# A linear attention and tanh-shrink MLP kernel: copies of v moved, epsilon ahead of den, transposes one step later, and the last output tile over two queues

## The chip, the cores and the metric

A run uses one core of one Trainium2 chip. The metric is the device time of one execution in microseconds. A profiled execution gives a span that is some 1.8 us shorter than the time of the same execution (294.0 and 295.8 for the kernel before). VectorE is called DVE in the profile, TensorE PE, ScalarE ACT and GpSimd POOL.

## The reference, cut to what matters

```python
q, k, v: (8, 8, 576, 64) f32      # batch, heads, sequence, head width
q_p, k_p = phi(q), phi(k)         # phi(x) = where(x > 0, x, exp(x) - 1) + 1
kv  = einsum('bhsd,bhse->bhde', k_p, v);  z = sum(k_p, axis=2)
num = einsum('bhsd,bhde->bhse', q_p, kv)
den = einsum('bhsd,bhd->bhs', q_p, z)[..., None] + 1e-06
x   = (num / den)                 # to (4608, 512): batch and sequence by heads and width
h   = x @ w_in                    # (4608, 512) @ (512, 2048)
out = (h - tanh(h)) @ w_out       # (4608, 2048) @ (2048, 512)
```

## The kernel before: the parts that matter

The 4608 rows are done in nine stages of 512 (c = 0 to 8). A stage is L1 (x @ w_in, 16 steps of four matmuls, then tanh on ScalarE and the subtraction on VectorE into `gT`) and L2 (`gT` @ w_out, 16 steps of four matmuls). The attention of the batches to come is hung into these steps: `s1[n]` after step n of L1, `s2[n]` after step n of L2. TensorE, VectorE, ScalarE and GpSimd are each given their own instructions in this program order. In the first stage L2 goes by quarters of w_out: steps 0 to 3 read the first quarter for the four output tiles, steps 4 to 7 the second, and so on.

```python
def a_kv(b, banks):                     # k'v and z by 192 columns: v and a block of ones
    ...                                 # 36 matmuls of 64x192, v_b holds v and the ones
def a_kv_cols(b, banks):                # by 136 columns: 128 of v, 8 of ones, from the copy vp
    ...                                 # 36 matmuls of 64x136
def a_vp(b, i):                         # the copy of v that a_kv_cols reads
    nc.vector.tensor_copy(vp[:, i, :, 0:128].rearrange(...), v_b[b % 2][:, 0:2, i])

# all loads are issued by GpSimd, in this order
load_q(0); load_k(0); load_v(0); [load_wi(g) for g in range(4)]
load_k(1); load_wo(0); load_q(1); ...; load_wo(1); load_v(1); load_wo(2)

# first stage (c == 0)
s2[1]: a_qphi(1, 1), load_q(2), load_wo(3), load_k(2), load_v(2)
s2[3]: a_qT_pe(1, 0)                    # transposes of q of batch 1, first half (nine on TensorE)
s2[4]: a_qT_pe(1, 1)                    # second half
s2[5]: b0_scale_rest, prepare;  s2[6]: a_kv(1);  s2[8]: a_den(1) ...
s2[15]: a_kphi(2, 0)
# second stage (c == 1)
s1[1]: a_kphi(2, 1);  s1[6]: a_kv(2);  s1[9]: a_den(2)
# each stage from c == 1 to 5: at s2[8] the copies of the batch after next, then num
s2[8]: a_qphi(n2, 1), a_qT_dma(n2), a_vp(n2, 0), a_vp(n2, 1)
s2[9..13] (c == 1: 11..15): a_num(n1, p)     # eviction by VectorE, two PSUM banks in turn
```

Of the kernel before, what the change touches and what calls it, by code (L numbers as in the profile page):

```python
# [18 lines left out]
def kernel(  # L19
# [9 lines left out]
    nc = tc.nc  # L29
    B, H, S, D = q.shape  # L30
    N = B * S
    DM = H * D
    DF = moe_w_in.shape[1]
    NP = H // 2
    NF = DF // 128
    NC = N // 512
    J = S // 64
# [105 lines left out]
    def a_kphi(b, i):  # L143
        phi(b, k_t, kp_t, "kp", i)

    def a_qphi(b, i):
        phi(b, q_t, qp_t, "qp", i)
# [4 lines left out]
    def a_qT_dma(b):  # L152
        new_qT(b)
        nc.sync.dma_start_transpose(
            out=qT_t[b].rearrange("p i j g t -> p (i j) (g t)"),
            in_=qp_t[b].rearrange("p i j h d -> p (i j h d)"))

    def a_qT_pe(b, i, banks, on=None):
        if i == 0:
            new_qT(b)  # L160
        for n in range(2):
            j0, j1 = ((0, 5), (5, 9))[n]
            ps = banks().bitcast(BF16).rearrange("p (j t) -> p j t", t=128)
            for j in range(j0, j1):
                nc.tensor.transpose(ps[:, j - j0, :], qp_t[b][:, i, j].rearrange("p h d -> p (h d)"), ident)  # L165
            src = ps[:, 0:j1 - j0, :]
            dst = qT_t[b][:, i, j0:j1].rearrange("p j g t -> p j (g t)")
            if (on or "AV")[n] == "A":
                nc.scalar.copy(dst, src)
            else:  # L170
                nc.vector.tensor_copy(dst, src)
# [14 lines left out]
        for hg in range(2):  # L186
            nc.vector.tensor_mul(kz_t[b][:, hg], ps[hg][:, :, 0:160], mask[:, hg])

    def a_vp(b, i):
        nc.vector.tensor_copy(vp[:, i, :, 0:128].rearrange("p j (h d) -> p h j d", h=2), v_b[b % 2][:, 0:2, i])  # L190

    def a_kv_cols(b, banks):
        kp = kp_t[b]
        kz_t[b] = kz_c[b % 2]
        ps = [banks()[:, 0:272].rearrange("p (i e) -> p i e", i=2) for hg in range(2)]
        for i in range(2):
            for j in range(J):
                for hg in range(2):
                    r = slice(64 * hg, 64 * hg + 64)
                    nc.tensor.matmul(ps[hg][:, i, :], kp[r, i, j].rearrange("p h d -> p (h d)"),  # L200
                                     vp[r, i, j, :], start=(j == 0), stop=(j == J - 1))
        for hg in range(2):
            nc.vector.tensor_mul(kz_t[b][:, hg, :, 0:136], ps[hg], mask[:, hg, :, 0:136])
# [61 lines left out]
            xT[:, :, 512:576].rearrange("p a (t c) -> p a t c", t=4),  # L265
            ps[:, 0:NP, :].rearrange("p a (t c) -> p a t c", t=4), rdb_t[0])

    def a_den(b, banks):

        kz, qT = kz_t[b], qT_t[b]  # L270
        ps = banks()[:, 0:J * 16]
        for n, p in enumerate((0, 2, 1, 3)):
            for t in range(4):
                nc.tensor.matmul(ps[32 * t:32 * t + 32], kz[:, p // 2, p % 2, 128:160],  # L274
                                 qT[:, p % 2, :, p // 2, 16 * t:16 * t + 16],
                                 start=(n == 0), stop=(n == NP - 1 and b > 0))
        for t in range(4) if b == 0 else ():
            nc.tensor.matmul(ps[32 * t:32 * t + 32], eps[:, 0:32], one[:, 0:J * 16], start=False, stop=True)
        if b > 0:
            den = rpool.tile([128, J * 16], F32, name="den")  # L280
            nc.vector.tensor_scalar(den, ps, 1e-6, None, ALU.add)
        else:
            den = ps
        rden = rpool.tile([128, J * 16], F32, name="rden")
        nc.vector.reciprocal(rden, den)  # L285
        rden_t[b] = rden
# [97 lines left out]
    def evac(c, i, o, f0=0, f1=None):  # L384
        f1 = DM if f1 is None else f1
        osb = opool.tile([128, DM], F32, name="osb")
        nc.scalar.copy(osb[:, f0:f1], o[:, f0:f1])  # L387
        for half in range(2):
            b, j = divmod(2 * (4 * c + i) + half, J)
            nc.sync.dma_start(out=out[b * S:(b + 1) * S, f0:f1].rearrange("(p j) m -> p j m", j=J)[:, j, :],  # L390
                              in_=osb[64 * half:64 * half + 64, f0:f1])


# [96 lines left out]
    for c in range(NC):  # L490
        gT = gpool.tile([128, NF, 512], BF16, name="gT")
        n1, n2 = c + 1, c + 2
        s1 = {i: [] for i in range(16)}
        s2 = {i: [] for i in range(16)}
        if c == 0:
            side = Banks([4, 5, 6, 7])
            sub = {}

            def spread1(h):
                sub["bp"] = a_spread_pe(1, 4, (2 * h, 2 * h + 1))  # L500
                for p in (2 * h, 2 * h + 1):
                    a_scale(1, p, sub["ns"], sub["bp"], 144 * (p % 2))

            def num1():
                sub["ns"] = new_ns(1)
                for p in (NP, 0, 1, 2, 3):
                    a_num_copy(1, sub["ns"], p, side)

            s1[11].append(lambda: a_kphi(1, 0))
            s1[13].append(lambda: a_kphi(1, 1))  # L510
            s2[0].append(lambda: a_qphi(1, 0))
            s2[1].append(lambda: (a_qphi(1, 1), load_q(2), load_wo(3), load_k(2), load_v(2)))
            s2[3].append(lambda: a_qT_pe(1, 0, side))
            s2[4].append(lambda: a_qT_pe(1, 1, side))
            s2[5].append(lambda: (b0_scale_rest(side), prepare()))
            s2[6].append(lambda: a_kv(1, side))
            s2[8].append(lambda: a_den(1, side))
            s2[9].append(lambda: (num1(), a_split(1)))
            s2[11].append(lambda: (spread1(0), a_qphi(2, 0)))
            s2[13].append(lambda: (spread1(1), a_qphi(2, 1), a_qT_dma(2)))  # L520
            s2[15].append(lambda: a_kphi(2, 0))
        elif n1 < B:
            s1[6 if c == 1 else 5].append(lambda: (a_kv if c == 1 else a_kv_cols)(n1, attn))
            s1[9 if c == 1 else 8].append(lambda: (a_den(n1, attn), a_spread(n1)))
            for p in range(NP + 1):
                s2[(11 if c == 1 else 9) + p].append(lambda p=p: a_num(n1, p))
        if c == 1:
            s1[1].append(lambda: a_kphi(2, 1))
        if c >= 1 and n2 < B:

            s1[0].append(lambda: (gate(gT, 0), load_k(n2), load_q(n2), load_v(n2)))
            d = 2
            s2[d].append(lambda: a_kphi(n2, 0))
            s2[d + 2].append(lambda: a_kphi(n2, 1))
            s2[d + 4].append(lambda: a_qphi(n2, 0))
            s2[d + 6].append(lambda: (a_qphi(n2, 1), a_qT_dma(n2), a_vp(n2, 0), a_vp(n2, 1)))
        if c == 0:

            first = Banks([4, 5, 6, 7, 0, 1, 2, 3])
            hs = [ps_all[:, n, :] for n in range(4)]  # L540
            order = [((0, 0), (0, 1)), ((2, 0), (2, 1), (0, 2), (0, 3), (2, 2), (2, 3)),
                     [(p, fi) for p in (1, 3) for fi in range(4)]]
            seen = [0] * 4
            for n, part_ in enumerate(order):
                if n == 1:
                    open2()
                for p, fi in part_:
                    l1mm(c, fi, hs[fi], p, seen[fi])
                    seen[fi] += 1
            for fi in range(4):  # L550
                l1act(fi, hs[fi], gT)
        for fi in range(4 if c == 0 else 0, NF):
            h = first() if c == 0 else dense()
            for p in range(NP):
                l1mm(c, fi, h, p, p)
            l1act(fi, h, gT)
            for f in s1[fi]:
                f()
        os_ = {}
        for s in range(16):  # L560

            (g, i) = divmod(s, 4) if c == 0 else (s % 4, s // 4)
            if g == 0:
                os_[i] = ps_all[:, i, :] if c == 0 else dense()
            if c == NC - 1 and i == 3:

                if g == 0:
                    o2 = dense()
                    for u, o in enumerate((os_[i], o2)):
                        f = slice(256 * u, 256 * u + 256)  # L570
                        for fi in range(NF):
                            nc.tensor.matmul(o[:, f], gT[:, fi, 384:512], w_out_sb[:, fi, f],  # L572
                                             start=(fi == 0), stop=(fi == NF - 1))
                        evac(c, i, o, 256 * u, 256 * u + 256)
                continue
            l2mm(gT, os_[i], i, 4 * g, 4 * g + 4)
            if g == 3:
                evac(c, i, os_[i])
            for f in s2[s]:
                f()  # L580
# [30 lines left out]
```

## Time and profile before

| | before |
|---|---|
| time, median of the first 3 runs | 295.23 us (295.14 to 295.88) |
| span of the profiled execution | 294.0 us |
| TensorE busy | 285.9 us, 97% |
| start of the second stage (its first L1 matmul in the chain) | 51.29 us |
| end of den of batch 2, inside the second stage | 61.98 us |
| end of the last matmul | 289.71 us |

The prediction shows the lines of the page, of the chain and of the timelines on which it rests. The lines of a timeline give start us, us, engine, line, operation.

```profile
21.01 0.75 POOL L116 DMA_DIRECT2D w_out_sb<-in_moe_w_out_dram  x1
```

The landing counts from the issue's start: the v load issued at 38.84 with 13.3 us to landing moves its last packets between 51.8 and 52.0, so just before 52.1.

### The profile page before, as it was taken

How to read it: one execution, taken by the hardware profiler on the slowest of the kernel's cores; microseconds unless marked ns; L12 is line 12 of the kernel's file. 1: busy time of each engine (PE TensorE's matmuls, PEld its weight loads, DVE VectorE, ACT ScalarE, POOL GpSimd, SP SyncE). 2: the span in 40 equal slices, each digit the busy share in tenths (PEclk: the TensorE clock that was granted, in tenths of full speed). 3: DMA queues.
4: the chain of work that ended last, by engine and by line, in shares of the span. 5: the costliest groups of instructions: out<-in, count | busy, mean ns of one | idle time of the engine just before them, and what ended most of it. 6: DMA issues, size and time to landing. Idle time of an engine off the chain costs nothing.

```text
span 294.0 us, 4681 instructions
## 1 busy us (share of the span) xinstructions
PE 285.9 (97%) x1801; PEld 134.9 (46%) x1801; DVE 182.3 (62%) x326; ACT 150.4 (51%) x233; POOL 31.9 (11%) x53
## 2 busy tenths in 40 slices
PE   7899999999999999999999999999999999999994
PEld 2444454544454444544444445444444444444443
DVE  4759967986668574877478557855780477018500
ACT  4848818856355644565356535752561166137421
POOL 8571030300030003000110003000000000000000
PEclk9999999999999999999999999999999999999999
DMA  6999999898959665957697679776117310230033
GB/s 106 189 205 213 208 207 217 150 219 157 230 100 208 151 150 101 202 128 167 132 175 151 151 147 143 142 180 135 38 35 166 71 37 0 50 82 13 2 71 71
DMA packets 38534, 38.95 MB, mean 132 GB/s; under 512 B 16304, under 2 KB 33264, under 8 KB 37744
## 3 DMA queue, kind: packets, MB, share of 16 engines
q0 software_dynamic: 17008, 18.35, 38.3%
q1 hardware_dynamic: 21504, 20.31, 30.6%
q8 instruction: 14, 0.23, 0.3%
q14 instruction: 8, 0.07, 0.1%
HBM read 43.91 MB, written 9.55 MB: 182 GB/s over the span
## 4 chain that ended last, share of the span: by engine, by line
PE 91%; DVE 3%; DMA 3%; POOL 1%; issue 1%; ACT 0%; DVEq 0%; POOLq 0%
PE ps_all L366 42%; PE ps_all L381 40%; DMA v<-in_v_dram 3%; PE ps_all L317 2%; PE ps_all L200 2%; PE ps_all L572 1%; PE ps_all L178 1%; DVE gT L372 1%; PE ps_all L274 1%; DVE kp L137 1%; PE ps_all L241 1%; POOL kraw L90 0%; POOL qraw L90 0%; PE ps_all L222 0%; PE ps_all L165 0%
## 5 line engine op out<-in xcount | busy, mean ns | idle before, releaser
L372 DVE TENSOR_TENSOR gT<-ps_all,th 128x512 bf16<-128x512 f32 x144 | 96.8, 687 | 51.0 <-ACT th L371 50.4
L366 PE MATMUL ps_all<-xT,w_in_sb 128*128 128x512 bf16 x576 | 128.0, 379 | 0.3 <-DVE xT L245 0.3
L381 PE MATMUL ps_all<-w_out_sb,gT 128*128 128x512 bf16 x560 | 128.1, 379 | 0.0
L371 ACT ACTIVATE th<-ps_all 128x512 f32<-128x512 f32 x144 | 85.1, 598 | 48.1 <-PE ps_all L366 43.0
L366 PEld LDWEIGHTS <-w_in_sb 128*128 128x128 bf16 x576 | 55.2, 98 | 66.7 <-issue 0.9
L381 PEld LDWEIGHTS <-gT 128*128 128x128 bf16 x560 | 53.9, 98 | 64.4 <-issue 1.2
L387 ACT COPY osb<-ps_all 128x512 f32<-128x512 f32 (+1 forms) x37 | 21.2, 575 | 77.2 <-PE ps_all L381 53.9
L328 DVE TENSOR_TENSOR xT<-ps_all,rdb 128x512 bf16<-128x512 f32 x24 | 15.8, 686 | 11.7 <-PE ps_all L317 11.7
L135 ACT ACTIVATE e<-qraw 128x1152 bf16<-128x1152 bf16 x16 | 18.5, 1163 | 3.8 <-DMA qraw<-in_q_dram 3.8
L137 DVE TENSOR_TENSOR kp<-e,r 128x1152 bf16<-128x1152 bf16 x15 | 11.4, 758 | 12.7 <-ACT e L135 11.8
L135 ACT ACTIVATE e<-kraw 128x1152 bf16<-128x1152 bf16 x15 | 17.4, 1163 | 0.6 <-DMA kraw<-in_k_dram 0.6
L137 DVE TENSOR_TENSOR qp<-e,r 128x1152 bf16<-128x1152 bf16 x16 | 12.1, 758 | 7.4 <-ACT e L135 6.5
L377 POOL COPY g<-gT 1x1 bf16<-1x1 bf16 x5 | 0.9, 176 | 124.4 <-DVE gT L372 124.4
L317 PE MATMUL ps_all<-qT,kz 128*128 128x512 bf16 x28 | 10.1, 379 | 0.0
L432 PE MATMUL ps_all<-zero 128*128 128x512 bf16 x29 | 8.6, 454 | 1.2 <-DVE zero L394 1.2
L136 DVE TENSOR_SCALAR r<-qraw 128x1152 bf16<-128x1152 bf16 x16 | 7.2, 453 | 2.2 <-DMA qraw<-in_q_dram 2.2
L285 DVE RECIPROCAL rden<-den 128x144 f32<-128x144 f32 x7 | 7.4, 1053 | 0.2
L136 DVE TENSOR_SCALAR r<-kraw 128x1152 bf16<-128x1152 bf16 x15 | 6.8, 451 | 0.1
L93 POOL DMA_DIRECT2D qraw<-in_q_dram x7 | 5.2, 748 | 14.6 <-DVE r L136 13.4
L200 PEld LDWEIGHTS <-kp 64*128 64x128 bf16 x180 | 5.3, 94 | 2.1 <-issue 2.1
L200 PE MATMUL ps_all<-vp,kp 64*128 64x136 bf16 x180 | 6.2, 220 | 0.0
L93 POOL DMA_DIRECT2D kraw<-in_k_dram x7 | 5.2, 749 | 3.7 <-issue 1.3
(79 smaller groups left out, 106.2 us busy)
## 6 DMA issues: line engine op xcount, KB each, us to landing
out_dram<-osb SPq DMA_DIRECT2D x70, 128.0 KB
rdb<-ds SPq DMA_DIRECT2D x12, 576.0 KB
kraw<-in_k_dram POOLq DMA_DIRECT2D x7, 576.0 KB, 6.0
qraw<-in_q_dram POOLq DMA_DIRECT2D x7, 576.0 KB, 8.1
v<-in_v_dram POOLq DMA_DIRECT2D x7, 576.0 KB, 10.8
w_in_sb<-in_moe_w_in_dram POOLq DMA_DIRECT2D x8, 256.0 KB, 10.5
w_out_sb<-in_moe_w_out_dram POOLq DMA_DIRECT2D x4, 512.0 KB, 14.1
qraw<-in_q_dram POOLq DMA_DIRECT2D x2, 288.0 KB, 4.7
```

The lines of the kernel that those rows point to most:

```text
L93: nc.gpsimd.dma_start(out=t.rearrange("q h i j d -> q (h i) (j d)"), in_=x.rearrange("(n q) x -> q n x", n=4))
L135: return (lambda: nc.scalar.activation(e, x, AF.Exp), lambda: nc.vector.tensor_scalar(r, x, 0.0, 1.0, ALU.max, ALU.add), lambda: nc.vector ...
L136: lambda: nc.vector.tensor_scalar(r, x, 0.0, 1.0, ALU.max, ALU.add),
L137: lambda: nc.vector.tensor_tensor(y, e, r, ALU.min))
L200: nc.tensor.matmul(ps[hg][:, i, :], kp[r, i, j].rearrange("p h d -> p (h d)"), vp[r, i, j, :], start=(j == 0), stop=(j == J - 1))
L317: nc.tensor.matmul(ps, kz[:, p // 2, p % 2, 0:128], qT[:, p % 2, 0:8, p // 2, :], start=True, stop=True)
L328: nc.vector.tensor_mul(xT[:, p, S * b:S * b + 512].rearrange("p (j t c) -> p j t c", j=8, t=4), ps.rearrange("p j (t c) -> p j t c", t=4), ...
L366: nc.tensor.matmul(h, w_in_sb[:, 2 * (p % 2) + p // 2, fi * 128:(fi + 1) * 128], xT[:, p, c * 512:(c + 1) * 512], start=(n == 0), stop=(n ...
L371: nc.scalar.activation(th, h, AF.Tanh)
L372: nc.vector.tensor_sub(gT[:, fi, :], h, th)
L381: nc.tensor.matmul(o, gT[:, fi, i * 128:(i + 1) * 128], w_out_sb[:, fi, :], start=(fi == 0), stop=(fi == NF - 1))
L387: nc.scalar.copy(osb[:, f0:f1], o[:, f0:f1])
```

## The change

The intent, part by part: (1) batch 2 takes the cheaper k'v of 136 columns too, its two copies made by GpSimd; (2) for batches 3 to 7 VectorE's copies stand behind num and not in front of it; (3) the epsilon matmuls of batch 0 run before the others of den, where TensorE waits anyway; (4) the transposes of batch 1 run one step later, so that TensorE has matmuls to do while q is on its way; (5) the last output tile is split into 384 and 128 columns, and the last of its four output DMAs is issued from ScalarE's queue.

```diff
-    def a_vp(b, i):
-        nc.vector.tensor_copy(vp[...], v_b[b % 2][:, 0:2, i])
+    def a_vp(b, i, eng):
+        eng.tensor_copy(vp[...], v_b[b % 2][:, 0:2, i])
 ...                                       # a_den: epsilon first, start/stop flags to match
+        for t in range(4) if b == 0 else ():
+            nc.tensor.matmul(ps[32 * t:32 * t + 32], eps[:, 0:32], one[:, 0:J * 16], start=True, stop=False)
 ...
-        for half in range(2):
+        for half, q_ in enumerate((nc.sync, nc.sync if f1 < DM or c < NC - 1 or i < 3 else nc.scalar)):
 ...
-            s2[3].append(lambda: a_qT_pe(1, 0, side))
-            s2[4].append(lambda: a_qT_pe(1, 1, side))
+            s2[4].append(lambda: a_qT_pe(1, 0, side))
+            s2[5].append(lambda: a_qT_pe(1, 1, side))
 ...
-            s2[15].append(lambda: a_kphi(2, 0))
+            s2[15].append(lambda: (a_kphi(2, 0), a_vp(2, 0, nc.gpsimd), a_vp(2, 1, nc.gpsimd)))
 ...
-            s1[6 if c == 1 else 5].append(lambda: (a_kv if c == 1 else a_kv_cols)(n1, attn))
+            s1[6 if c == 1 else 5].append(lambda: a_kv_cols(n1, attn))
 ...
-            s2[d + 6].append(lambda: (a_qphi(n2, 1), a_qT_dma(n2), a_vp(n2, 0), a_vp(n2, 1)))
+            s2[d + 6].append(lambda: (a_qphi(n2, 1), a_qT_dma(n2)))
+            for i in range(2):
+                s2[14 + i].append(lambda i=i: a_vp(n2, i, nc.vector))
 ...
-                    for u, o in enumerate((os_[i], o2)):
-                        f = slice(256 * u, 256 * u + 256)
+                    for o, f in ((os_[i], slice(0, 384)), (o2, slice(384, DM))):
```

More of the change, by code (lines that the diff above doesn't have):

```diff
@@ L187, in a_kv @@
             nc.vector.tensor_mul(kz_t[b][:, hg], ps[hg][:, :, 0:160], mask[:, hg])
-    def a_vp(b, i):
-        nc.vector.tensor_copy(vp[:, i, :, 0:128].rearrange("p j (h d) -> p h j d", h=2), v_b[b % 2][:, 0:2, i])
+    def a_vp(b, i, eng):
+        eng.tensor_copy(vp[:, i, :, 0:128].rearrange("p j (h d) -> p h j d", h=2), v_b[b % 2][:, 0:2, i])
     def a_kv_cols(b, banks):
@@ L266, in b0_scale_rest, with a_den @@
             ps[:, 0:NP, :].rearrange("p a (t c) -> p a t c", t=4), rdb_t[0])
-    def a_den(b, banks):
+    def a_den(b, banks, parts=range(4)):
         kz, qT = kz_t[b], qT_t[b]
         ps = banks()[:, 0:J * 16]
+        for t in range(4) if b == 0 else ():
+            nc.tensor.matmul(ps[32 * t:32 * t + 32], eps[:, 0:32], one[:, 0:J * 16], start=True, stop=False)
         for n, p in enumerate((0, 2, 1, 3)):
-            for t in range(4):
-                nc.tensor.matmul(ps[32 * t:32 * t + 32], kz[:, p // 2, p % 2, 128:160],
-                                 qT[:, p % 2, :, p // 2, 16 * t:16 * t + 16],
-                                 start=(n == 0), stop=(n == NP - 1 and b > 0))
-        for t in range(4) if b == 0 else ():
-            nc.tensor.matmul(ps[32 * t:32 * t + 32], eps[:, 0:32], one[:, 0:J * 16], start=False, stop=True)
+            if n in parts:
+                for t in range(4):
+                    nc.tensor.matmul(ps[32 * t:32 * t + 32], kz[:, p // 2, p % 2, 128:160],
+                                     qT[:, p % 2, :, p // 2, 16 * t:16 * t + 16],
+                                     start=(n == 0 and b > 0), stop=(n == NP - 1))
         if b > 0:
@@ L387, in evac @@
         nc.scalar.copy(osb[:, f0:f1], o[:, f0:f1])
-        for half in range(2):
+        for half, q_ in enumerate((nc.sync, nc.sync if f1 < DM or c < NC - 1 or i < 3 else nc.scalar)):
             b, j = divmod(2 * (4 * c + i) + half, J)
-            nc.sync.dma_start(out=out[b * S:(b + 1) * S, f0:f1].rearrange("(p j) m -> p j m", j=J)[:, j, :],
+            q_.dma_start(out=out[b * S:(b + 1) * S, f0:f1].rearrange("(p j) m -> p j m", j=J)[:, j, :],
                               in_=osb[64 * half:64 * half + 64, f0:f1])
@@ L573 @@
                                              start=(fi == 0), stop=(fi == NF - 1))
-                        evac(c, i, o, 256 * u, 256 * u + 256)
+                        evac(c, i, o, f.start, f.stop)
                 continue
```

## The prediction

> **What bounds the kernel now.** I read the page first, then the chain of work that ended last in order of time, then the table of waits, and last the timelines of single engines around each place that the change touches. The page and the chain:
>
> ```profile
> PE 285.9 (97%) x1801; PEld 134.9 (46%) x1801; DVE 182.3 (62%) x326; ACT 150.4 (51%) x233; POOL 31.9 (11%) x53
> ...
> PE 91%; DVE 3%; DMA 3%; POOL 1%; issue 1%; ACT 0%; DVEq 0%; POOLq 0%
> ```
>
> TensorE is busy for 286 of 294 us, and the chain runs over it for 91% of the span. From 35.8 us to 289.7 us the chain in order of time has nothing but PE pieces, one after the other. So in that stretch only two things can shorten the kernel: fewer TensorE cycles, or a stall that hides inside a PE piece. Outside it there are the opening (up to 35.8 us) and the tail (4 us after the last matmul). The pieces of that view that the change concerns (start us, us, what):
>
> ```profile
> 13.72 0.31 PE ps_all L274 x8
> 14.03 0.06 PE ps_all L278 x4
> ...
> 57.33 1.59 PE ps_all L178 x36
> ...
> 87.24 1.17 PE ps_all L200 x36
> ...
> 107.33 0.22 PE ps_all L317
> 107.55 0.86 PE ps_all L381 x4
> 108.41 0.36 PE ps_all L317
> ...
> 286.20 3.51 PE ps_all L572 x32
> 289.71 0.02 issue
> 289.73 0.37 ACT osb L387
> ```
>
> The reader is to see: batch 2 forms k'v with 192 columns per matmul (L178, 1.59 us) where later batches use 136 (L200, 1.17 us); one num matmul takes 0.36 us where its neighbours take 0.22; the den of batch 0 has four epsilon matmuls after its last real one; and the tail is two 256-column groups, a ScalarE copy, and then 3.9 us of output DMA. One stall of TensorE itself stands in its own timeline just before the transposes of batch 1 (L165):
>
> ```profile
> 31.59 3.62 PE L381 MATMUL ps_all<-w_out_sb,gT 128*128 128x512 bf16 x16
> 35.80 0.68 PE L165 MATMUL ps_all<-ident,qp 128*128 128x128 bf16 x9 [0.59 <-DVE qp L137]
> 36.31 1.03 PE L381 MATMUL ps_all<-w_out_sb,gT 128*128 128x512 bf16 x4
> 37.18 0.67 PE L165 MATMUL ps_all<-ident,qp 128*128 128x128 bf16 x9
> ```
>
> [...] 0.86 us for four of 512, 3.51 us for 32 of 256 (110 ns). [...] No GpSimd copy of this size is in the trace; its memset of 128x1152 bf16 took 1.08 us, VectorE's vp copy of that size 453 ns. [...] an output DMA's issue takes 0.47 to 0.60 us on the SP queue, one after the other.
>
> **The change part by part.**
>
> Epsilon ahead of den (batch 0). The program order shows the four matmuls moved in front of the sixteen, with a wait on VectorE that is already met (the bank's previous reader is the first z copy, at 12.65 us). There TensorE waits anyway: eight den matmuls at 13.22 us, then 0.19 us idle for the second z copy. So 0.06 us leaves the path. What follows is the reciprocal (14.14, 1.06 us), whose end starts the spreads at 15.35; they come 0.06 earlier. Gain 0.06.
>
> Transposes one step later (batch 1). Now 16 matmuls of L2 start at 31.59 and by 216 ns each end issuing at 35.05; TensorE then waits for qp until 35.80 (0.75 us), and the first group of nine transposes takes 0.68 where the second takes 0.50 in the chain (0.18 for its exposed start). After: four more L2 matmuls run first (35.05 to 35.91; qp's first half is ready at 35.74), then nine transposes (0.50), four matmuls (0.86, to 37.27; qp's second half is ready at 36.98), nine transposes. No wait is left: gain 0.75+0.18 = 0.93. Against it: the L2 step that first reads the fourth quarter of w_out starts at 47.38 now and would start at 46.4, and that quarter's DMA is issued at 37.37 and takes 9.1 us to landing, 46.5. Its trigger is VectorE's read of qraw, which does not move. Estimated wait 0.1. Net 0.83.
>
> Batch 2 by columns (a_kv becomes a_kv_cols): 1.59 - 1.17 = 0.42 of pure TensorE time. Gain 0.42. It needs vp for batch 2, two copies of 128x1152, now on GpSimd. v of batch 2 is issued at 38.84 and lands 13.3 us later, 52.1. By the memset I estimate 1.1 to 1.2 us per copy, so vp is complete at 54.5[...]. TensorE asks for it at 57.3 - 0.9 = 56.4. Enough[...]. In the other direction VectorE's kp TENSOR_TENSOR[...] falls due at about 52.3 and can be held for one copy, about 1.1 us. Its next deadlines: the first gT of that stage must free its bank by 55.5 (it would be done at 54.6), the second half of kp must be there by 56.9 (it would be at 56.5). Expected cost 0.1.
>
> Copies behind num (batches 3 to 7). Before, two copies stand between qp and the first num eviction:
>
> ```profile
> 106.92 0.82 DVE L190 COPY vp<-v 128x1152 bf16<-128x1152 bf16 x2
> 107.66 1.88 DVE L328 TENSOR_TENSOR xT<-ps_all,rdb 128x512 bf16<-128x512 f32 x3
> ```
>
> The first eviction ends at about 108.35, and the third num matmul, which has the same bank (two banks rotate), starts at 108.39 instead of 108.25. That is the 0.36 instead of 0.22. It stands in the chain four times (108.41, 138.91, 169.41, 199.90); in the stage of batch 2 the copies stand three steps ahead of num, and the stage of batch 7 has none, and both show 0.22. After, the first eviction begins 0.7 us earlier and the stall is gone: 4 x 0.14 = 0.56. The moved copies run at the end of the stage or between the last two evictions, where VectorE is otherwise idle. Gain 0.56.
>
> Tail. [...] The last copy: 586 ns for 512 columns and 373 for 256 give 0.83 ns per column, so about 267 ns for 128, 0.10 less. DMA: now the last two issues on SP start at 290.1 and 290.6, the end is 3.4 us after the last. After, the copy of 384 columns ends at about 289.3, its two issues hold SP until about 290.4, then SP issues one 128-column half; the other half goes from ACT at about 290.0. The last issue thus starts 0.2 earlier and moves half the bytes (32 instead of 64 KB), another 0.1 to 0.2. I take 0.35 in all.
>
> Sum: 0.06 + 0.83 + 0.42 - 0.10 + 0.56 + 0.35 = **2.12 us**, from 295.2 to **293.1 us**, 0.7%.
>
> **The rivals.**
>
> A. GpSimd copies are slow. At 2.4 us per copy (twice the estimate) kp would be held until 54.5, the second copy would end at 57.7, and the second half of kp[...] would come at about 58.8 where TensorE wants it at 56.9. That is a new stall of about 2 us at batch 2's k'v, and the whole comes to 295. For it: VectorE is packed from 47.5 to 60 us. Against it: the 1.08 us memset[...]. Chance about 15%.
>
> B. The opening's 0.93 turns into a wait for w_out. The DMA's queue is full from 30 to 51 us (over 200 GB/s), the margin is zero, and a landing half a microsecond later gives 293.6; if all is eaten, 294.0. Chance of more than 0.4 lost: 25%.
>
> C. The tail gains nothing. The SP queue now has two issues of 384 columns right before its last[...]. Then 293.5. Chance 30%; a loss of 0.3 is possible.
>
> D. Nothing is gained at num because something else holds the third matmul. Against it: the two stages without copies directly before num show no stall. Then 293.7; chance 7%.
>
> **Range and chances.** All gains add on TensorE's path, since from 51 to 286 us nothing but TensorE is on it. B and C together pull the mean to about 293.3, A has a tail up to 295.5; on the other side 292.5 needs w_out on time, no cost at GpSimd and 0.6 in the tail. The three runs before spread over 0.7 us. Predicted 293.2 us, range 292.4 to 294.4. A change of 2% would be 5.9 us: no sum of these parts gives it, and the worst rivals together stop about at the old time. Faster 0.01, same 0.98, slower 0.01.
>
> **What would show each step right or wrong.** The timeline of PE around 35 us: 20 matmuls of L2 before the first transposes and no wait for qp (right); a wait of the L2 matmuls near 46.5 us for w_out (rival B). The chain: at batch 2 a piece of 36 matmuls of L200 with 1.17 us in place of 1.59; all num pieces at 0.21 to 0.22. The group of GpSimd copies: mean 1.1 to 1.3 us (right), over 2 (A), and then a wait of L200 for POOL or kp, or VectorE instructions much longer than 758 ns between 52 and 56 us. The tail: from the end of the last matmul to the end of the span about 3.9 us instead of 4.3. The prediction is wrong if the sum of PE's busy time and its stalls between 51 and 286 us does not fall by about 1.0 us, or the start of the second stage (51.29 us) by 0.8 to 0.9.

The 32 matmuls took 3.51 us in both profiles. Of the 0.10 for batch 2 the reason is gone why a GpSimd copy should hold VectorE: no trace had shown a hold when this was written, and its length of 1.1 us is the author's estimate from the memset. The runs below do show one (TENSOR_SCALAR 1.40 us instead of 0.45, TENSOR_TENSOR 1.51 instead of 0.76). Between the page and the parts are times of the trace before: matmuls (the 28 of 512 columns at 51.29 us take 6.04 us, so 216 ns each), GpSimd's memset, VectorE's copy, and the issues on the SP queue. The 0.1 to 0.2 us for half the bytes are an estimate as well: the packets of one 64 KB piece moved for some 0.4 us (291.25 to 291.7).

## More of the kernel before

```profile
L116 POOL DMA_DIRECT2D w_out_sb<-in_moe_w_out_dram x1: 747/747/747, 21.0 to 21.0; - x1
...
DMA to landing us min/median/max: 14.7/14.7/14.7
```

The second quarter of w_out is issued at 21.01 us (GpSimd's timeline) and lands 14.7 us later (the view of the tile w_out for that one issue), at 35.7.

## The result, and the profile after

| | before | after |
|---|---|---|
| time, median of 6 runs | 295.41 us (295.14 to 295.97) | 295.18 us (295.00 to 295.52) |
| ratio | | 0.9991 (95%: 0.9978 to 1.0004) |
| span of the profiled execution | 294.0 us | 293.7 us |
| start of the second stage | 51.29 us | 51.62 us |
| from there to the end of den of batch 2 | 10.69 us | 10.91 us |
| from the third stage's start to the seventh's | 121.98 us | 121.42 us |
| from the last matmul to the end | 4.29 us | 4.01 us |

Of 2.1 us expected some 0.3 came (0.23 by the medians), and the interval of the ratio holds 1. The parts in the table add up: 0.33 and 0.22 lost, 0.56 and 0.28 gained, together 0.29 against the 0.3 by which the spans differ. So two of the five parts did not just fail; they cost time. The page after, its busy times and its chain:

```profile
PE 285.4 (97%) x1801; PEld 134.1 (46%) x1801; DVE 183.9 (63%) x326; ACT 150.6 (51%) x233; POOL 34.6 (12%) x55
...
PE 81%; DMA 9%; DVE 5%; POOL 3%; issue 1%; ACT 0%; DVEq 0%; POOLq 0%
```

TensorE has 10 points less of the chain than before; DMA (6), VectorE (2) and GpSimd (2) have taken them. Where, the timelines tell. First TensorE's around the transposes; its lines answer to the four that the prediction shows from before:

```profile
30.82 3.62 PE L382 MATMUL ps_all<-w_out_sb,gT 128*128 128x512 bf16 x16
36.14 1.02 PE L382 MATMUL ps_all<-w_out_sb,gT 128*128 128x512 bf16 x4 [1.70 <-DMA w_out_sb<-in_moe_w_out_dram]
```

The wait for qp is gone, and in its place stands one of 1.70 us for w_out: the four matmuls put ahead of the transposes read its second quarter, and that lands at 36.1 us. (TensorE came to this point 0.8 us earlier than in the profile before. The opening varies that much by itself: the 16 matmuls started between 30.7 and 32.2 us in the eleven further profiles below.)

Then the second stage. The timeline of all engines in the profile after, with GpSimd's two copies merged into one line, and the two VectorE lines of the same work from VectorE's timeline before:

```profile
52.59 2.78 POOL L190 COPY vp<-v 128x1152 bf16<-128x1152 bf16 x2 [13.22 <-DMA v<-in_v_dram]
52.97 1.40 DVE L136 TENSOR_SCALAR r<-kraw 128x1152 bf16<-128x1152 bf16 x1
...
54.48 1.51 DVE L137 TENSOR_TENSOR kp<-e,r 128x1152 bf16<-128x1152 bf16 x1
...
58.47 0.71 PE L200 MATMUL ps_all<-vp,kp 64*128 64x136 bf16 x18 [0.17 <-DVE kp L137]
```

```profile
52.64 0.45 DVE L136 TENSOR_SCALAR r<-kraw 128x1152 bf16<-128x1152 bf16 x1
53.19 0.76 DVE L137 TENSOR_TENSOR kp<-e,r 128x1152 bf16<-128x1152 bf16 x1
```

The same two instructions take 1.40 and 1.51 us instead of 0.45 and 0.76: 1.70 us more. The two copies, asked for one by one, take 1.46 and 1.36 us. The first runs to about 54.05, and the TENSOR_SCALAR ends 0.3 us after that; the second runs to about 55.35, and the TENSOR_TENSOR ends 0.6 us after that. VectorE was held twice in a row. TensorE feels it at k'v (a wait of 0.17 us for kp) and at den, whose kz comes late: its 16 matmuls take 0.72 us where they took 0.43.

Where the copies moved behind num, the chain shows what was predicted; the lines answer to those at 107.33 to 108.41 before:

```profile
107.88 0.22 PE ps_all L318
108.10 0.86 PE ps_all L382 x4
108.96 0.22 PE ps_all L318
```

### The profile page after: what moved, and what is told of

The parts are those of the page before. It is cut to its first block, busy times and chain, and to the rows that moved or that the text cites. A ratio compares the mean times of both kernels' runs of the same rounds, so it can differ in the third digit from the quotient of the medians. Undisturbed runs are those within 1.5% of the kernel's fastest.

```text
span 293.7 us, 4685 instructions
## 1 busy us (share of the span) xinstructions
PE 285.4 (97%) x1801; PEld 134.1 (46%) x1801; DVE 183.9 (63%) x326; ACT 150.6 (51%) x233; POOL 34.6 (12%) x55
## 4 chain that ended last, share of the span: by engine, by line
PE 81%; DMA 9%; DVE 5%; POOL 3%; issue 1%; ACT 0%; DVEq 0%; POOLq 0%
PE ps_all L382 39%; PE ps_all L367 35%; DMA w_out_sb<-in_moe_w_out_dram 5%; DMA w_in_sb<-in_moe_w_in_dram 4%; PE ps_all L318 2%; PE ps_all L200 2%; DVE gT L373 1%; PE ps_all L575 1%; DVE xT L360 1%; PE ps_all L277 1%; DVE r L136 1%; DVE kp L137 1%; POOL v L409 1%; PE ps_all L178 1%; DVE qp L137 1%
## 5 line engine op out<-in xcount | busy, mean ns | idle before, releaser
L388 ACT COPY osb<-ps_all 128x512 f32<-128x512 f32 (+2 forms) x37 | 21.2, 574 | 76.5 <-PE ps_all L382 59.8
L329 DVE TENSOR_TENSOR xT<-ps_all,rdb 128x512 bf16<-128x512 f32 x24 | 16.5, 690 | 14.2 <-PE ps_all L318 14.2
L137 DVE TENSOR_TENSOR kp<-e,r 128x1152 bf16<-128x1152 bf16 x15 | 12.1, 809 | 12.5 <-ACT e L135 11.6
L200 PE MATMUL ps_all<-vp,kp 64*128 64x136 bf16 x216 | 7.6, 220 | 0.2 <-DVE kp L137 0.2
L136 DVE TENSOR_SCALAR r<-kraw 128x1152 bf16<-128x1152 bf16 x15 | 7.7, 514 | 0.0
L200 PEld LDWEIGHTS <-kp 64*128 64x128 bf16 x216 | 6.4, 94 | 2.9 <-issue 2.5
L93 POOL DMA_DIRECT2D qraw<-in_q_dram x7 | 5.2, 748 | 14.7 <-DVE r L136 12.3
```

The lines of the kernel that those rows point to most:

```text
L93: nc.gpsimd.dma_start(out=t.rearrange("q h i j d -> q (h i) (j d)"), in_=x.rearrange("(n q) x -> q n x", n=4))
L136: lambda: nc.vector.tensor_scalar(r, x, 0.0, 1.0, ALU.max, ALU.add),
L137: lambda: nc.vector.tensor_tensor(y, e, r, ALU.min))
L200: nc.tensor.matmul(ps[hg][:, i, :], kp[r, i, j].rearrange("p h d -> p (h d)"), vp[r, i, j, :], start=(j == 0), stop=(j == J - 1))
L329: nc.vector.tensor_mul(xT[:, p, S * b:S * b + 512].rearrange("p (j t c) -> p j t c", j=8, t=4), ps.rearrange("p j (t c) -> p j t c", t=4), ...
L388: nc.scalar.copy(osb[:, f0:f1], o[:, f0:f1])
```

## The experiments

Eleven runs were made, two of the kernels as they are and nine of variants. All times are medians; the ratios are to the kernel before in the same rounds. The runs fall into three groups of rounds, each on a chip of its own: before again, transposes back, k'v back and w_out free; then after again, copies unused, copies behind num and VectorE copies late; then the other three. The kernel before took 295.43, 295.43 and 295.65 us in them. One of its eleven times in the third group is 297.16 us; without it the three ratios of that group would be about 0.0005 higher. "Start" is the start of the second stage, "stretch" is from there to the end of den of batch 2, both from the chain; where the chain is not on TensorE at that place, the start is TensorE's timeline plus 0.16 or 0.17 us, by which the two views differ in the other profiles (51.12 and 51.29 before). The changed kernel was timed in other rounds than the runs compared with it; it had 295.18 us in both of its own, against 295.41 and 295.43 for before.

| run | time us | ratio (95%) | start us | stretch us |
|---|---|---|---|---|
| before again | 295.71 | 1.0006 (0.9993 to 1.0019) | 51.33 | 10.69 |
| after again | 295.18 | 0.9997 (0.9984 to 1.0009) | 51.36 | 10.90 |
| transposes back | 294.25 | 0.9964 (0.9950 to 0.9977) | 50.83 | 10.28 |
| k'v of batch 2 back | 294.93 | 0.9982 (0.9969 to 0.9994) | 51.45 | 10.70 |
| w_out free (wrong result) | 294.32 | 0.9961 (0.9948 to 0.9973) | 51.16 | 10.28 |
| copies unused | 295.45 | 1.0002 (0.9989 to 1.0014) | 51.65 | 11.01 |
| copies behind num only | 294.77 | 0.9984 (0.9972 to 0.9997) | 50.80 | 10.69 |
| VectorE copies, late | 294.98 | 0.9989 (0.9975 to 1.0002) | 50.90 | 11.11 |
| transposes moved only | 295.75 | 1.0004 (0.9985 to 1.0023) | 51.14 | 10.69 |
| tail only | 295.37 | 0.9987 (0.9970 to 1.0004) | 50.96 | 10.70 |
| VectorE copies, early | 294.22 | 0.9950 (0.9933 to 0.9967) | 50.89 | 10.27 |

### The kernel before, once more

No edit.

> The kernel before once more, unchanged: how much the opening and the time vary by themselves. If the opening varies (the first k'v of batch 0 started at 12.39 us in the profile before and at 11.66 in the one after, though nothing ahead of it was changed), this profile shows another value than 12.39, while the start of the second stage (51.29) moves by less than 0.4 us. Ratio to before 1.000 within 0.002.

The ratio is 1.0006. The first k'v of batch 0 started at 12.42 us, so this profile did not itself show the spread that I asked about; the others do. A difference of a tenth of a per cent between two kernels is within what the same kernel shows.

### The transposes put back

```diff
 # in the kernel after
-            s2[4].append(lambda: a_qT_pe(1, 0, side))
-            s2[5].append(lambda: a_qT_pe(1, 1, side))
+            s2[3].append(lambda: a_qT_pe(1, 0, side))
+            s2[4].append(lambda: a_qT_pe(1, 1, side))
```

> The changed kernel with only the transposes of batch 1 put back one step. Theory W (the second quarter of w_out, landing at 35.7 to 36.1 us, is what the moved L2 step waits for, so moving gained almost nothing and exposed a later landing): the wait of 1.7 us for w_out is gone or short, a wait for qp of 0.5 to 1 us is back, the second stage starts at 51.2 to 51.4 instead of 51.62, time equal to the changed kernel's or up to 0.3 us below. Rival (the move did gain 0.9 us, and something else in the opening lost it): second stage starts at 52.2 to 52.6, time 0.7 to 0.9 us above the changed kernel's.

The time fell by 0.93 us below the changed kernel, more than theory W allowed (up to 0.3) and opposite to its rival. TensorE's timeline of this run:

```profile
30.67 3.62 PE L382 MATMUL ps_all<-w_out_sb,gT 128*128 128x512 bf16 x16
35.28 0.68 PE L165 MATMUL ps_all<-ident,qp 128*128 128x128 bf16 x9 [0.99 <-DVE qp L137]
35.86 1.02 PE L382 MATMUL ps_all<-w_out_sb,gT 128*128 128x512 bf16 x4
```

Nine transposes fit into the time in which TensorE has to wait for w_out in any case (issued at 21.60 us in this run, 14.2 us to landing, so 35.8). Waiting for qp costs nothing there. In the profiles the start comes 0.79 us earlier, of which 0.51 are the nine transposes and 0.28 an earlier landing; another 0.63 lies in the second stage, whose stretch fell from 10.91 to 10.28 us. (That makes 1.42 us and not 0.93: the profiled executions took 295.46 and 294.04 us, one slower and one faster than its kernel's median.) The engines' timeline there:

```profile
52.19 0.45 DVE L136 TENSOR_SCALAR r<-kraw 128x1152 bf16<-128x1152 bf16 x1
52.30 2.96 POOL L190 COPY vp<-v 128x1152 bf16<-128x1152 bf16 x2 [13.21 <-DMA v<-in_v_dram]
...
52.74 1.51 DVE L137 TENSOR_TENSOR kp<-e,r 128x1152 bf16<-128x1152 bf16 x1
```

VectorE's TENSOR_SCALAR got in 0.11 us ahead of the first copy and was not held; only the TENSOR_TENSOR was, by 0.75 us, and that reached nobody. The stage starts earlier by 0.8 us than in the profile after while v lands 0.3 us earlier, so VectorE's pair stands differently against the copies. The two losses thus look tied: the later opening turned one hold into two. All five profiles with GpSimd copies fit this. In three the TENSOR_SCALAR starts 0.38 to 0.41 us after the first copy and two instructions are held; in two it starts 0.11 and 0.49 us before, and one is held.

### k'v of batch 2 put back

```diff
 # in the kernel after
-            s2[15].append(lambda: (a_kphi(2, 0), a_vp(2, 0, nc.gpsimd), a_vp(2, 1, nc.gpsimd)))
+            s2[15].append(lambda: a_kphi(2, 0))
-            s1[6 if c == 1 else 5].append(lambda: a_kv_cols(n1, attn))
+            s1[6 if c == 1 else 5].append(lambda: (a_kv if c == 1 else a_kv_cols)(n1, attn))
```

> The changed kernel with batch 2 as in the kernel before: k'v with 192 columns and no GpSimd copies. Theory G (the GpSimd copies hold VectorE for 1.7 us, and that delay reaches TensorE at k'v and den of batch 2 and costs more than the 0.42 us of columns): from the start of the second stage to the end of its den the time falls from 10.91 to 10.7 us, no wait for kp or kz there, kp instructions at 758 ns again, time 0.2 us below the changed kernel's. Rival (the copies cost TensorE nothing, the columns are a true gain): that stretch grows to 11.3 us and the time is 0.4 us above.

As theory G had it: the stretch is 10.70 us, no wait is left in it, and the time is 0.25 us below the changed kernel's. In the changed kernel part (1) is a loss, of 0.21 us by the stretch; the intervals of the two ratios overlap, so the timing alone does not show it. This run also shows how the opening is pinned: its 16 matmuls began 1.4 us later than in the profile after (32.18 against 30.82), and yet the second stage starts 0.17 us earlier, because w_out landed slightly earlier (the next four matmuls, which wait for it in both profiles, start at 35.98 us against 36.14).

### L2 without the wait for w_out (wrong result)

```diff
 # in the kernel after, l2mm with an argument back=0 and w_out_sb[:, fi - back, :]
-            l2mm(gT, os_[i], i, 4 * g, 4 * g + 4)
+            l2mm(gT, os_[i], i, 4 * g, 4 * g + 4, 4 if c == 0 and g == 1 else 0)
```

> The changed kernel, wrong result on purpose: in the first stage's second quarter L2 reads the first quarter of w_out, which has long landed, instead of the second. Theory W: the wait of 1.7 us before the moved step disappears, TensorE runs on to the transposes, the second stage starts at about 50.4 to 50.7 instead of 51.62 (it may then wait for the third or last quarter of w_out, near 41 or 46.5 us, for up to 0.3 us), and the time falls by about 0.8 to 1.0 us. Rival (the wait was for qp or a bank, or what is gained is lost again further on): less than 0.3 us.

The result is wrong as intended (relative error 0.17). The wait is gone and the time falls by 0.86 us. That this is the figure of theory W is partly luck: it was to come from the start alone, and the second stage starts at 51.16 and not at 50.4 to 50.7. TensorE's timeline shows what caught it:

```profile
38.91 1.66 PE L178 MATMUL ps_all<-v,kp 64*128 64x192 bf16 x36 [0.33 <-DMA v<-in_v_dram]
...
47.21 1.89 PE L382 MATMUL ps_all<-w_out_sb,gT 128*128 128x512 bf16 x8 [0.53 <-DMA w_out_sb<-in_moe_w_out_dram]
```

It waits for v of batch 1 and then for the last quarter of w_out. A TensorE freed of one load meets the next one. The second of these is rival B of the prediction: 0.53 us, where the prediction reckoned 0.1. In the changed kernel no such wait is left, since the second quarter held TensorE first. In the profiles 0.46 us of the gain lie in the start and 0.63 in the stretch (10.28 us): VectorE met the copies with one instruction only. The engines' timeline there, with the two copies in one line:

```profile
51.96 0.46 DVE L136 TENSOR_SCALAR r<-kraw 128x1152 bf16<-128x1152 bf16 x1
...
52.45 2.76 POOL L190 COPY vp<-v 128x1152 bf16<-128x1152 bf16 x2 [13.18 <-DMA v<-in_v_dram]
...
52.88 1.32 DVE L137 TENSOR_TENSOR kp<-e,r 128x1152 bf16<-128x1152 bf16 x1 [0.47 <-ACT e L135]
```

Asked for one by one, the copies take 1.14 and 1.67 us. The first starts with VectorE idle (from 52.42 to 52.88), the only one of the ten copies in all profiles that does. The other nine, 1.34 to 1.67 us, each overlap a VectorE instruction that either ran when they started or had been waiting for the copy ahead. So 1.14 us is the best figure for the copy itself; why the others took longer is not shown, since this is read from the order of the records (GpSimd's are rough) and was not tested by a run of its own.

### The changed kernel, once more

No edit.

> The changed kernel once more, unchanged: are its two losses there in a second execution? Theory W: w_out's second quarter lands at 35.7 to 36.1 us again, the matmuls of the moved step start within 0.1 us of that, the transposes come after it, and the second stage starts 15.5 us after the landing (15.5 in the profile of after, 15.0 where the transposes were put back). Theory P[...]: the first GpSimd copy starts at 52.3 to 52.8; if VectorE's first kraw TENSOR_SCALAR of the stage comes after that start, two VectorE instructions are held, about 1.7 us in all, and the stretch from the second stage's start to the end of den takes 10.7 to 11.0 us; if it comes before, one is held, 0.75 us, and the stretch takes 10.3. Ratio to before 0.999 within 0.0015.

Both losses are there again: the matmuls of the moved step start at 35.88 us (issue at 21.6 and 14.2 us to landing), and VectorE's instructions take 1.40 and 1.51 us, with the first copy at 52.30 and the TENSOR_SCALAR at 52.71. The stretch is 10.90 us. Theory P's rule on who comes first is met.

### The GpSimd copies made but not used

```diff
 # in the kernel after; the GpSimd copies stay
-            s1[6 if c == 1 else 5].append(lambda: a_kv_cols(n1, attn))
+            s1[6 if c == 1 else 5].append(lambda: (a_kv if c == 1 else a_kv_cols)(n1, attn))
```

> The changed kernel with k'v of batch 2 by 192 columns as before, but the two GpSimd copies still made, unused: the cost of the copies without their gain. Theory P: VectorE's instructions are held as in the changed kernel (one at 1.3 to 1.5 us instead of 0.45 or 0.76, or two); where two are, the stretch from the second stage's start to the end of den takes 10.9 to 11.3 us, against 10.70 without copies, and the time is 0.2 to 0.5 us above that of the run with 192 columns and no copies (0.9982 of before). Rival (the copies hold nobody that matters, and the run without copies was faster by chance): the stretch takes 10.7 us and the time is that of the run without copies.

Two VectorE instructions held again (1.40 and 1.51 us), the stretch is 11.01 us against 10.70 without copies, and the time is 0.52 us above that of the run without copies (ratios 1.0002 and 0.9982). The only difference between the two kernels is two GpSimd instructions whose result nobody reads. Of the 0.52 us, 0.31 lie in the stretch and are the cost of the hold on VectorE; 0.20 lie in the start (51.65 against 51.45), before the copies run, and are w_out's landing. The two runs were made in different groups, and their intervals overlap a little; the stretch and the held instructions carry the proof, not the time.

### The copies behind num, alone

```diff
 # in the kernel before
-            s2[d + 6].append(lambda: (a_qphi(n2, 1), a_qT_dma(n2), a_vp(n2, 0), a_vp(n2, 1)))
+            s2[d + 6].append(lambda: (a_qphi(n2, 1), a_qT_dma(n2)))
+            for i in range(2):
+                s2[14 + i].append(lambda i=i: a_vp(n2, i))
```

> The kernel before with only the copies of batches 3 to 7 moved behind num. Theory (the step of the prediction that looks right): the four num pieces of 0.36 us become 0.22, VectorE's first eviction starts 0.7 us earlier, time 0.56 us below before, ratio 0.998. Rival: something else takes the time back, ratio above 0.9993.

Ratio 0.9984 (0.9972 to 0.9997), which is 0.47 us; from the third stage's start (81.57 us) to the seventh's (202.99) it takes 121.42 us against 121.98 before. That is the predicted 0.56 to the hundredth, and no num piece of 0.36 us is left: the step holds.

### The copies of batch 2 by VectorE, first place

```diff
 # in the kernel after, transposes back, GpSimd's copies out
+            s1[3].append(lambda: (a_vp(2, 0, nc.vector), a_vp(2, 1, nc.vector)))
```

> The changed kernel with the transposes put back and the copies for batch 2 by VectorE (453 ns each) at the fourth step of the second stage, behind the kp work that GpSimd held. Theories W and P: no VectorE instruction of 1.3 us and more there, second stage starts at 50.8 to 51.3, the stretch to the end of den takes 10.3 us, the time is at or up to 0.2 us below that of the run with the transposes back (0.9964 of before). Rival (VectorE's own 0.9 us in that packed place delays gT and kz as much as GpSimd did): the stretch takes 10.6 us and more, the time is above 0.997 of before.

A miss: 0.9989. TensorE's timeline:

```profile
57.63 1.32 PE L200 MATMUL ps_all<-vp,kp 64*128 64x136 bf16 x36 [0.68 <-DVE vp L190]
```

VectorE runs behind in this stage. In its program order the two copies stood behind the second half of kp and two more gT, and they came at 57.12 us, when TensorE was already there. The rival of that expectation was right in its stretch (11.11 us) and wrong in its reason: neither gT nor kz was late, but the copies.

### The transposes moved, alone

```diff
 # in the kernel before
-            s2[3].append(lambda: a_qT_pe(1, 0, side))
-            s2[4].append(lambda: a_qT_pe(1, 1, side))
+            s2[4].append(lambda: a_qT_pe(1, 0, side))
+            s2[5].append(lambda: a_qT_pe(1, 1, side))
```

> The kernel before with only the transposes of batch 1 moved one step later: the step of the prediction that was to bring 0.83 us net. Theory W: no wait for qp any more, but one for w_out's second quarter (35.7 to 36.1 us), the transposes and their evictions come after it, the second stage starts 15.5 us after that landing, at 51.2 to 51.6, and the time is that of before or up to 0.4 us above, ratio 1.000 to 1.0015. Rival (the predicted gain is there and another part loses it): second stage at 50.4 to 50.6, ratio 0.997 to 0.998.

Ratio 1.0004 (0.9985 to 1.0023): the predicted 0.83 us, a ratio of 0.9972, is not there without the other parts either. TensorE waits 1.08 us for w_out, whose matmuls start at 35.66. The second stage starts 15.48 us later, at 51.14, just below the range that was expected, because w_out landed early in this run (35.6).

### The tail, alone

```diff
 # in the kernel before: the 384 and 128 columns and the second queue, as in the change
```

> The kernel before with only the last tile as 384 and 128 columns over two queues. From the end of the last matmul to the end of the span 4.0 us instead of 4.3 (as in the profile of after), time 0.2 to 0.4 us below before, ratio 0.999. Rival: within 0.1 us of before.

From the last matmul to the end of the span 4.0 us again. The ratio, 0.9987, has the right sign and about the right size, but its interval holds 1. That the tail gains 0.3 us is thus shown by the two profiles and not by the timing. No run separates the second queue from the smaller last piece.

### The copies of batch 2 by VectorE, two steps earlier

```diff
 # in the kernel after, transposes back, GpSimd's copies out
-            s1[1].append(lambda: a_kphi(2, 1))
+            s1[1].append(lambda: (a_vp(2, 0, nc.vector), a_vp(2, 1, nc.vector), a_kphi(2, 1)))
```

> As the candidate, but VectorE's two copies for batch 2 stand ahead of the second half of kp, two steps earlier. The candidate waited 0.7 us at k'v for these copies, which came at 57.1 us behind two gT. Theory: now they run at 54 to 55 us, the wait at k'v is gone, the stretch from the second stage's start to the end of den takes 10.3 us, no VectorE instruction is held, and the time is that of the run with the transposes back (0.9964 of before) or up to 0.3 us below the candidate's 0.9989 at the least. Rival (kp's second half now comes late): a wait for kp at k'v, stretch above 10.5 us, ratio above 0.998.

The wait at k'v is gone and the stretch is 10.27 us. VectorE's timeline:

```profile
54.67 0.82 DVE L190 COPY vp<-v 128x1152 bf16<-128x1152 bf16 x2
55.41 0.45 DVE L136 TENSOR_SCALAR r<-kraw 128x1152 bf16<-128x1152 bf16 x1
55.96 0.76 DVE L137 TENSOR_TENSOR kp<-e,r 128x1152 bf16<-128x1152 bf16 x1
```

At 294.22 us and 0.9950 of before it beats both kernels: the change without its moved transposes, and with the copies on VectorE. The ratios do not separate it from the run with the transposes back and the copies still on GpSimd (294.25 us, 0.9964); there one hold was free.

## Why the prediction was wrong

**The transposes (predicted gain 0.83 us net; none came).** The failing sentence is "After: four more L2 matmuls run first (35.05 to 35.91)". I checked that their gT was there and that the transposes' qp would be, and I checked the landing of the fourth quarter of w_out. I did not check the second quarter, which these very matmuls are the first to read. Its landing, 35.7 us, was in the profile before; it did not show as a wait because TensorE was at that time waiting for qp and then transposing. The gap in front of that step had two causes, and the profile puts it down to the one that ended last, by 0.1 us. In the changed kernel the four matmuls waited 1.70 us, until 36.14.

The start of those matmuls and the start of the second stage tell it in all profiles but that of the wrong-result run, which has no such wait. Where the transposes were moved, they start at 36.14, 35.88, 35.98, 36.17 and 35.66 us, and the second stage 15.48 us later each time (15.47 once). Where they were not moved, they start at 36.31, 36.35, 35.86, 35.83, 35.93, 35.99 and 35.92, and the second stage 14.97 or 14.98 us later. Moving gained nothing at the start (means 35.97 and 36.03) and put nine transposes, 0.51 us, behind it. The second stage starts at 51.44 us in the mean of the five moved and at 51.00 in that of the seven others: a loss of 0.44 us where a gain of 0.83 was predicted. The loss is a mean over profiles of one execution each, and the times of the move alone (1.0004) exclude the gain without showing the loss. Its size depends on which of the two waits ends last. In the profile before, where qp did, the step's 15.48 us after a landing at 35.7 would have given 51.2 instead of 51.29, about even; where w_out does, as in the run with the transposes back, the whole 0.51 us is lost.

**Batch 2 by columns (predicted gain 0.42, cost 0.10; the cost was mis-sized).** The gain is real: where VectorE is held once or not at all, the stretch is 10.27 or 10.28 us instead of 10.69. The term that failed is the cost. I reckoned 1.1 to 1.2 us for a copy and one hold of 1.1 us, which the deadlines could bear (the lengths were estimates from the memset; no trace had shown a hold). The copy's own time was about right (1.14 us where VectorE was idle at its start, against 1.08 for the memset of that size and 0.45 for VectorE's copy). The number of holds was wrong: in the changed kernel the two copies held two VectorE instructions in turn, 0.95 and 0.75 us, 1.70 in all. The prediction had watched the TENSOR_TENSOR only, not the TENSOR_SCALAR before it. That raised the stretch by 0.63 us, to 10.91, more than the columns save. Rival A named the hold but asked only for the copy's speed; what went with two holds or one in all five profiles was who came first, by 0.1 to 0.5 us, and in the changed kernel VectorE came second because its stage started late. With the early start that the prediction counted on, its cost of 0.10 would have been enough: with one hold the stretch is as short as with none. So this failure hangs on the first, and so does the sentence "All gains add on TensorE's path": in the profile after, the chain runs over VectorE from 47.84 to 62.11 us.

**Copies behind num (predicted 0.56).** Right: 0.56 in the profile, 0.47 in time when done alone (0.1 to 0.8 by the interval). The reading of one 0.36 us piece among 0.22 us pieces was sound. Rival D falls.

**The tail (predicted 0.35).** About right, 0.28 in size. The 128-column copy took 0.27 us as worked out; how the rest divides between the earlier issue and the smaller piece is not shown. The issue from ScalarE's queue took 0.56 us, the last ones on SP 0.47 to 0.60. Rival C falls, by the profiles.

**Epsilon (predicted 0.06).** Right where it stands: in the profile after the epsilon matmuls start at 12.49 us and the others of den at 12.56, and VectorE's reciprocal waits 0.41 us for den instead of 0.48. From the start of the second z copy to that of the reciprocal it takes 0.63 or 0.64 us in all eight profiles with this part and 0.69 to 0.71 in all five without. But where the opening ends at a DMA landing, as in the changed kernel, those 0.06 us do not reach the end.

Replacing the two failed terms gives -0.44 - 0.21 + 0.56 + 0.28 = 0.2 us gained, where the medians show 0.23 (here -0.44 is the mean over profiles and -0.21 is 0.42 less 0.63). With an interval of about 0.4 us to either side that agreement proves little. Rival B named the right kind of wait, but for the wrong quarter of w_out; the one for the last quarter came only in the run in which the second was taken away. Both tests that the prediction set for itself failed: the start of the second stage went from 51.29 to 51.62 us instead of 0.8 to 0.9 earlier, and from there to the last 32 matmuls (286.20 and 286.18) it took 0.35 us less instead of about 1.0.

What stays open: why the opening varies by 1.5 us between executions of the same program up to there. Nor was an order of loads tried that brings the second quarter of w_out sooner; the run without that wait suggests that v of batch 1 and the last quarter would then take over.

## What to carry to other kernels

Before moving work up into an idle gap, look up every operand of that work for its own time of arrival, above all loads that a busy DMA queue is still delivering (here 14.7 us from issue to landing, at a mean of 209 GB/s from 20 to 36 us); a gap that ends with one wait can hide another that ends close to it (0.1 us here), and then the work that already stands in the gap is free and should stay. Copies moved to GpSimd to relieve VectorE can hold VectorE for longer than VectorE would have taken itself (1.70 us against two times 0.45 here); put them where the hold reaches nobody (the single one of 0.75 us did not: 10.28 us for the stretch), or leave them on VectorE and place them by the order in which the results are due. A part that loses can hide a part that wins: test the parts one by one even when the sum is "the same".
